# Block-decay attention ahead of two dense stages: the x products grouped by matmul shape, x in two PSUM banks

## The chip, the cores and the metric

The kernel runs on one core of a Trainium2 chip. Its engines work side by side: TensorE (PE, with its weight loads as PEld), VectorE (DVE), ScalarE (ACT), GpSimd (POOL), and SyncE (SP), which issues the DMAs. The metric is device time in microseconds of a whole execution; less is better.

## The reference

Attention with a decaying state over blocks, then two dense stages on its result:

```python
# q, k, v: [2, 8, 768, 64] float32; lam: [8], one decay per head
intra = einsum('bhic,bhjc->bhij', qb, kb) * Dmask        # Dmask = lam^(i-j) for j <= i, else 0
intra = einsum('bhij,bhjd->bhid', intra, vb)
inter = einsum('bhid,bhde->bhie', qb * lam_pow, kv_state)
out   = intra + inter
kv_state = lam_block * kv_state + einsum('bhsd,bhse->bhde', kb * rev_pow, vb)
...
x = attention as [1536 tokens, 512]
h = x @ w_in;  g = max(0.01 h, h);  y = g @ w_out         # w_in 512x2048, w_out 2048x512
a = y @ w1;  b = y @ w2;  out = (a * b) @ w3 @ w_out2      # 512x1024 twice, 1024x1024, 1024x512
```

The dense weights come as float64.

## The kernel before, in words

Tokens come in chunks of 128, twelve in all: chunks 0 to 5 are the first batch row, 6 to 11 the second. Chunks 0 and 6 start with an empty state (no state product), 5 and 11 hand none on (no outer product). Four chunks make a group of 512 tokens; three groups go through the dense stages. The eight heads lie as four pairs p with two heads j each; a pair fills 128 rows of 64 channels per head.

A chunk (`attention`, from line 345) has these steps. *Scores* (line 370): per pair and head a product with 64 contraction rows, the head's j going to PSUM buffer j. *Mask* (373, VectorE): scores times the decay table, for each j. *q decay* (382) and *k decay* (391, two instructions, one per j), on VectorE or GpSimd. *x products* (`outs`): per pair, line 408 multiplies the state (128x128, the two heads' 64x64 states on its diagonal, zeros elsewhere) with the decayed q, and line 411 adds v times the masked scores, one product per head, each to 64 of the 128 output rows. All of x of a chunk lies in one PSUM buffer. *x parts* (425 on ScalarE, 155 on VectorE): x is split into a rounded part and the rest, both kept for the dense stages. *Outer product* (436): per pair k x v as 128x128, of which the two diagonal 64x64 blocks are used. *Fade* (443, GpSimd): the old state, 128x512, times the decay. *Update* (453, or 455 for an empty state): two instructions, one per head of a pair, 64 rows each.

float32 products (attention) appear in the profile as two TensorE records each; the dense stages use rounded float32, one record each.

A step h(f) of the dense part is 12 products of 128x512 (line 467), y(f) as well (474); a group has 16 of each. Weights are loaded, converted from float64 words by ScalarE (227) and VectorE (231, 237, 251), split into rounded part and rest (151, 155), all beside the first group's products. The y step needs the activation of its h step: a scaled copy (502, ScalarE), a maximum (505, VectorE), a rounded part (482, ScalarE) and a rest (155, VectorE).

The order of all instructions is made ahead of time by `in_order`: each engine takes the first step in rank that is ready by the planner's own prices. Buffers come from rings handed out in turn. The ring `ps` has four PSUM buffers: scores take two, x products one, the outer product one, an h step one, held until the rest of its activation is made. `qd` and `kd` have one buffer each.

## Time and profile before

| what | value |
|---|---|
| median of three timed runs | 579.96 us (579.31 to 581.09) |
| span of the profiled execution, its own time as far as the profile gives it | 577.9 us |
| TensorE busy | 564.4 us, 98% |
| VectorE busy | 367.0 us, 64% |
| ScalarE busy | 316.5 us, 55% |
| GpSimd busy | 131.8 us, 23% |

Busy shares are means over stages with different limits. TensorE's matmuls are pipelined, so durations of single records overlap; the distance between the starts of one kind of block and the next tells what a block takes. An idle time is listed with what ended it.

### The profile page before, as it was taken

How to read it: one execution, taken by the hardware profiler on the slowest of the kernel's cores; microseconds unless marked ns; L12 is line 12 of the kernel's file. 1: busy time of each engine (PE TensorE's matmuls, PEld its weight loads, DVE VectorE, ACT ScalarE, POOL GpSimd, SP SyncE). 2: the span in 40 equal slices, each digit the busy share in tenths (PEclk: the TensorE clock that was granted, in tenths of full speed). 3: DMA queues.
4: the chain of work that ended last, by engine and by line, in shares of the span. 5: the costliest groups of instructions: out<-in, count | busy, mean ns of one | idle time of the engine just before them, and what ended most of it. 6: DMA issues, size and time to landing. Idle time of an engine off the chain costs nothing.

```text
span 577.9 us, 7411 instructions
## 1 busy us (share of the span) xinstructions
PE 564.4 (98%) x2752; PEld 458.3 (79%) x2752; DVE 367.0 (64%) x572; ACT 316.5 (55%) x531; POOL 131.8 (23%) x111
## 2 busy tenths in 40 slices
PE   5899999999999999999999999999999999999997
PEld 5668788787887878788888888888888888888885
DVE  7989899999544467553466999988435333333330
ACT  2366777677633346474466887887335333343332
POOL 2332202323223123112243241021002111111100
PEclk9999999999999999999999999999999999999999
DMA  8746745785210313110032444653001000020001
GB/s 301 278 151 218 254 148 186 245 283 200 75 70 19 109 56 110 47 63 0 1 113 69 146 146 152 212 182 111 0 1 67 7 0 1 0 74 0 1 1 73
DMA packets 19188, 60.25 MB, mean 104 GB/s; under 512 B 2256, under 2 KB 2256, under 8 KB 19152
## 3 DMA queue, kind: packets, MB, share of 16 engines
q1 hardware_dynamic: 19152, 59.78, 30.1%
q8 instruction: 21, 0.34, 0.2%
q14 instruction: 15, 0.12, 0.1%
HBM read 54.53 MB, written 5.24 MB: 103 GB/s over the span
## 4 chain that ended last, share of the span: by engine, by line
PE 88%; issue 4%; DVE 3%; DMA 2%; POOL 1%; SPq 0%; ACT 0%; DVEq 0%; POOLq 0%
PE ps L467 43%; PE acc L474 32%; PE ps L585 8%; PE ps L411 2%; PE ps L408 2%; PE ps L436 1%; DMA inp<-in_qkv_dram 1%; PE ps L370 1%; DMA yf<-in_qkv_dram 1%; POOL wp L155 1%; DVE kd L391 1%; DVE rp L231 0%; DVE u L237 0%; DVE state L453 0%; DVE xy L155 0%
## 5 line engine op out<-in xcount | busy, mean ns | idle before, releaser
L467 PE MATMUL ps<-xy,wp 128*128 128x512 f32 x1152 | 275.4, 390 | 0.9 <-DVE xy L155 0.9
L467 PEld LDWEIGHTS ps<-xy,wp 128*128 128x128 f32 x1152 | 215.5, 188 | 46.6 <-DVE xy L155 1.3
L474 PE MATMUL acc<-act,wp 128*128 128x512 f32 x576 | 140.6, 392 | 0.2 <-POOL wp L155 0.2
L474 PEld LDWEIGHTS acc<-act,wp 128*128 128x128 f32 x576 | 107.0, 188 | 24.6 <-issue 0.7
L155 DVE TENSOR_TENSOR act<-ps,act 128x512 fp32r<-128x512 f32 x72 | 49.6, 690 | 37.2 <-ACT act L482 37.1
L474 PE MATMUL acc<-wp,act 128*128 128x512 f32 x288 | 69.0, 389 | 0.0
L227 ACT ACTIVATE rp<-raw,bp 128x512 f32<-128x512 uint16 x72 | 55.0, 764 | 22.9 <-DVE f L251 11.1
L474 PEld LDWEIGHTS acc<-wp,act 128*128 128x128 f32 x288 | 54.1, 188 | 11.2
L227 ACT ACTIVATE rn<-raw,bn 128x512 f32<-128x512 uint16 x72 | 54.8, 763 | 14.6 <-DVE rp L231 10.4
L151 ACT CAST wp<-f_w 128x512 fp32r<-128x512 f32 x48 | 29.5, 621 | 55.4 <-PE ps L467 46.3
L482 ACT CAST act<-ps 128x512 fp32r<-128x512 f32 x72 | 42.1, 585 | 25.8 <-DVE ps L505 18.8
L151 ACT CAST wp<-f_in 128x512 fp32r<-128x512 f32 x48 | 29.8, 620 | 44.7 <-PE ps L467 42.1
L231 DVE SCALAR_TENSOR_TENSOR rp<-rp,rn 128x512 uint32<-128x512 f32 x72 | 51.3, 713 | 0.8 <-ACT rp L227 0.7
L155 POOL TENSOR_TENSOR wp<-f_w,wp 128x512 fp32r<-128x512 f32 x18 | 23.3, 1296 | 117.2 <-ACT wp L151 89.6
L155 DVE TENSOR_TENSOR wp<-f_in,wp 128x512 fp32r<-128x512 f32 x29 | 22.9, 790 | 42.6 <-ACT wp L151 42.5
L155 DVE TENSOR_TENSOR wp<-f_w,wp 128x512 fp32r<-128x512 f32 x30 | 23.0, 772 | 35.1 <-ACT wp L151 35.1
L237 DVE TENSOR_SCALAR u<-raw 128x512 uint32<-128x512 uint32 x72 | 43.2, 600 | 0.2
L155 POOL TENSOR_TENSOR wp<-f,wp 128x512 fp32r<-128x512 f32 x16 | 22.5, 1408 | 69.2 <-ACT wp L151 68.1
L155 POOL TENSOR_TENSOR wp<-f_in,wp 128x512 fp32r<-128x512 f32 x19 | 25.1, 1321 | 54.8 <-ACT wp L151 54.8
L505 DVE TENSOR_TENSOR ps<-ps,ta 128x512 f32<-128x512 f32 x48 | 33.3, 693 | 4.0 <-ACT ta L502 3.8
L151 ACT CAST wp<-f 128x512 fp32r<-128x512 f32 x40 | 24.9, 621 | 18.9 <-PE acc L474 5.6
L619 DVE TENSOR_TENSOR ps<-ps,ta 128x512 f32<-128x512 f32 x24 | 16.8, 698 | 28.9 <-PE ps L467 28.9
(71 smaller groups left out, 518.1 us busy)
## 6 DMA issues: line engine op xcount, KB each, us to landing
inp<-in_qkv_dram SPq DMA_DIRECT2D x20, 512.0 KB, 5.4
raw<-in_w_in_dram SPq DMA_DIRECT2D x16, 512.0 KB, 4.4
raw<-in_w_out_dram SPq DMA_DIRECT2D x16, 512.0 KB, 4.4
raw<-in_w3t_dram SPq DMA_DIRECT2D x16, 512.0 KB, 3.7
raw<-in_w_dram SPq DMA_DIRECT2D x16, 512.0 KB, 3.3
raw<-in_wo_dram SPq DMA_DIRECT2D x8, 512.0 KB, 3.7
f<-out SPq DMA_DIRECT2D x16, 256.0 KB, 2.6
out_dram<-f SPq DMA_DIRECT2D x12, 256.0 KB, 2.1
```

The costliest lines, as they stand in the source:

```text
L151: return lambda e: nc.scalar.copy(dst(), src())
L155: engines[e].tensor_tensor(out=dst(), in0=src(), in1=hi_().bitcast(F32), op=ALU.subtract)
L227: nc.scalar.activation(out=new(buf, [P, 512]), in_=top, func=AF.Relu, scale=8.0, bias=T_[bias])
L231: nc.vector.scalar_tensor_tensor(out=rp.tile.bitcast(U32), in0=rp.tile, scalar=32768.0, in1=rn.tile, op0=ALU.min, op1=ALU.add)
L237: nc.vector.tensor_scalar(out=new(u, [P, 512], U32), in0=mid, scalar1=2.0**-13, scalar2=2.0**19 - 1, op0=ALU.mult, op1=ALU.min)
L408: nc.tensor.matmul(ps[:, p, :], T_["state", n % 2][:, p, :], qd.tile[:, p, :], start=True, stop=False)
L467: nc.tensor.matmul(o, w(a)[:, cc * P : (cc + 1) * P], x(b, cc), start=k == 0, stop=k == 3 * NCC - 1)
L474: nc.tensor.matmul(o, st(a), mv(b), start=first and k == 0, stop=last and k == 2)
L482: nc.scalar.copy(buf.tile[:, 0, :], ps.tile)
L505: nc.vector.tensor_tensor(out=ps.tile, in0=ps.tile, in1=ta.tile, op=ALU.max)
L585: nc.tensor.matmul(ps.tile, w(a)[:, k * P : (k + 1) * P], wos[j // 2][:, 2 * (j % 2) + b, :], start=j == 0 and n == 0, stop=j == NF2 - 1 a ...
L619: lambda e: nc.vector.tensor_tensor(out=pb.tile, in0=pb.tile, in1=ta.tile, op=ALU.mult),
```

## The change

The x products come in two blocks: first all products with the state, as 64x64 pieces of the array (64 rows by the head j, 64 columns by the half t of the output), in an order in which four neighbours lie in four different pieces; then all products with v, whose neighbours alternate between the output halves. x lies in two PSUM buffers by the head's parity j, each 128x256; its parts are made by two instructions each on ScalarE and VectorE. The state holds the 64x64 blocks alone (128 rows by 4 x 64 columns), so the zeroed squares go, fade handles 256 columns instead of 512, and the update is one instruction of 128x256. The outer product is eight products of 64x64 instead of four of 128x128. The k decay is one instruction over all heads, from a small table (`last`) that two small copies on VectorE fill. The rows of w_in are permuted on the host to fit the new channel order of x. The planner's prices for these steps change, and with them the order.

```diff
@@ pool_consts, mask_table
-            T_["state", j] = const.tile([P, NPAIR, P], F32, tag="w34_7" if j else "state0", name=f"state{j}")
-            nc.gpsimd.memset(T_["state", j], 0.0)
-        T_["faded"] = const.tile([P, NPAIR, P], F32, name="faded")
+            T_["state", j] = const.tile([P, NPAIR, D], F32, name=f"state{j}")
+        T_["faded"] = const.tile([P, NPAIR, D], F32, name="faded")
...
+            if j == 0:
+                T_["last"] = const.tile([P, NPAIR, 2], F32, name="last")
+            nc.vector.tensor_copy(T_["last"][:, :, j : j + 1], T_["dm", j][:, :, CH - 1 : CH])
@@ attention
-        s = op({"pe": 1750}, scores, rank, [ld[0]], [*pss, *a], [inp])
+        s = op({"pe": 1000}, scores, rank, [ld[0]], [*pss, *a], [inp])
...
-                new(kd, [P, NPAIR, 2, D])
-                for j in range(2):
-                    engines[e].tensor_tensor(
-                        out=kd.tile[:, :, j, :],
...
-                        in1=T_["dm", j][:, :, CH - 1 : CH].to_broadcast([P, NPAIR, D]), op=ALU.mult,
+                engines[e].tensor_tensor(
+                    out=new(kd, [P, H, D]), in0=inp.tile[:, 2, :].rearrange("q (h d) -> q h d", d=D),
+                    in1=T_["last"].rearrange("q p j -> q (p j)").unsqueeze(2).to_broadcast([P, H, D]), op=ALU.mult,
+                )
...
-        px = Buf("ps")
+        px = [Buf("ps"), Buf("ps")]
+        heads = [(s, t, j) for s in range(2) for j in range(2) for t in range(2)]
...
-            for p in range(NPAIR):
-                if inter:
-                    nc.tensor.matmul(ps[:, p, :], T_["state", n % 2][:, p, :], qd.tile[:, p, :], start=True, stop=False)
-                for j in range(2):
-                    h = 2 * p + j
+            if inter:
+                for s, t, j in heads:
+                    p = 2 * s + t
                     nc.tensor.matmul(
-                        ps[j * D : (j + 1) * D, p, :], inp.tile[:, 3, h * D : (h + 1) * D], a[j].tile[:, p, :],
-                        start=not inter, stop=True,
+                        px[j].tile[half[t], s, :], T_["state", n % 2][half[j], p, :], qd.tile[half[j], p, :],
+                        start=s == 0, stop=False, skip_group_check=True,
                     )
+            for s, t, j in heads:
+                p = 2 * s + t
+                h = 2 * p + j
+                nc.tensor.matmul(
+                    px[j].tile[half[t], s, :], inp.tile[:, 3, h * D : (h + 1) * D], a[j].tile[:, p, :],
+                    start=not inter and s == 0, stop=True, skip_group_check=True,
+                )
...
-            {"pe": 2170 if inter else 1300}, outs, rank + 2, [*masked, ld[1], *need], [px, xs[g]] if c == 0 else [px],
+            {"pe": 1700 if inter else 1100}, outs, rank + 2, [*masked, ld[1], *need],
+            [*px, xs[g]] if c == 0 else px, [inp, *a, *([qd] if inter else [])],
...
-        o1 = op({"act": 520}, x_hi, rank + 2, [xo], [], [px, xs[g]])
+        for j in range(2):
+            part = lambda v, j=j: xs[g].tile[:, v, j::2, sl]
...
+            o1 = op({"act": 390}, x_hi, rank + 2, [xo], [], [px[j], xs[g]])
...
-                    nc.tensor.matmul(
-                        ps[:, p, :], kd.tile[:, p, :, :].rearrange("q h d -> q (h d)"),
-                        inp.tile[:, 3, p * P : (p + 1) * P], start=True, stop=True,
-                    )
+                    for j in range(2):
+                        h = 2 * p + j
+                        nc.tensor.matmul(
+                            ps[j * D : (j + 1) * D, p, :], kd.tile[:, h, :], inp.tile[:, 3, h * D : (h + 1) * D],
+                            start=True, stop=True,
+                        )
...
-                for j in range(2):
-                    r = slice(j * D, (j + 1) * D)
-                    st, ps = T_["state", (n + 1) % 2][r, :, r], pst.tile[r, :, r]
...
-                        nc.vector.tensor_tensor(out=st, in0=ps, in1=T_["faded"][r, :, r], op=ALU.add)
+                st = T_["state", (n + 1) % 2]
...
+                    nc.vector.tensor_tensor(out=st, in0=pst.tile, in1=T_["faded"], op=ALU.add)
```

How instructions move, at three places. The first is TensorE at chunk 9, from its scores on; before:

```order
L370 MATMUL ps<-inp 128x128 x8
L436 MATMUL ps<-inp,kd 128x128 x4
L467 MATMUL ps<-xy,wp 128x512 x12
L408 MATMUL ps<-qd,state_112 128x128
L411 MATMUL ps<-a_1789,inp 64x128
L411 MATMUL ps<-a_1790,inp 64x128
...
L474 MATMUL acc<-act,wp 128x512 x12
```

The same place with the change:

```order
L372 MATMUL ps<-inp 128x128 x8
L451 MATMUL ps<-inp,kd 64x64 x8
L480 MATMUL ps<-xy,wp 128x512 x12
L413 MATMUL ps<-qd,state_111 64x128 x8
L420 MATMUL ps<-a_1860,inp 64x128 x2
L420 MATMUL ps<-a_1861,inp 64x128 x2
...
L487 MATMUL acc<-act,wp 128x512 x12
```

The four turns of one state product and two v products have become a block of eight state products and a block of eight v products; the steps around them keep their places.

The second is TensorE from the v products of chunk 6 to the scores of chunk 7; before:

```order
L411 MATMUL ps<-a_822,inp 64x128
L411 MATMUL ps<-a_823,inp 64x128
L474 MATMUL acc<-act,wp 128x512 x12
L370 MATMUL ps<-inp 128x128 x8
L467 MATMUL ps<-xy,wp 128x512 x12
```

The same place with the change:

```order
L420 MATMUL ps<-a_835,inp 64x128 x2
L420 MATMUL ps<-a_836,inp 64x128 x2
L487 MATMUL acc<-act,wp 128x512 x24
L480 MATMUL ps<-xy,wp 128x512 x36
L487 MATMUL acc<-act,wp 128x512 x12
L480 MATMUL ps<-xy,wp 128x512 x12
...
L372 MATMUL ps<-inp 128x128 x8
```

Chunk 7's scores stand twelve h and y steps later behind chunk 6's x products than before, where one y step stood between.

The third is VectorE at the start, behind the decay tables (`yf` holds the inputs of chunks 0 and 1, `inp` those of later ones); before:

```order
L391 TENSOR_TENSOR kd<-yf_115,dm_118 128x4x64
L391 TENSOR_TENSOR kd<-yf_115,dm_123 128x4x64
L373 TENSOR_TENSOR a_132<-ps,dm_118 128x512
L373 TENSOR_TENSOR a_133<-ps,dm_123 128x512
L455 COPY state_112<-ps 64x4x64 x2
L391 TENSOR_TENSOR kd<-yf_128,dm_118 128x4x64
L391 TENSOR_TENSOR kd<-yf_128,dm_123 128x4x64
L155 TENSOR_TENSOR xy<-ps,xy 128x4x128
L373 TENSOR_TENSOR a_179<-ps,dm_118 128x512
L373 TENSOR_TENSOR a_180<-ps,dm_123 128x512
L453 TENSOR_TENSOR state_110<-ps,faded 64x4x64 x2
```

The same place with the change:

```order
L375 TENSOR_TENSOR a_133<-ps,dm_116 128x512
L375 TENSOR_TENSOR a_134<-ps,dm_123 128x512
L384 TENSOR_TENSOR qd<-yf_129,lpow 128x512
L155 TENSOR_TENSOR xy<-ps,xy 128x2x128 x2
L468 COPY state_111<-ps 128x256
L375 TENSOR_TENSOR a_185<-ps,dm_116 128x512
L375 TENSOR_TENSOR a_186<-ps,dm_123 128x512
L466 TENSOR_TENSOR state_110<-ps,faded 128x256
```

The k decays are gone from VectorE here; with the change GpSimd does them for every chunk, those of chunks 0 and 1 as its first work behind the constants, and the q decay of chunk 1 has come to VectorE.

## Rows read from the trace of the kernel before

**Rows 1.** The page's first part: busy time, share and count by engine.
```profile
PE 564.4 (98%) x2752; PEld 458.3 (79%) x2752; DVE 367.0 (64%) x572; ACT 316.5 (55%) x531; POOL 131.8 (23%) x111
```

**Rows 2.** By stage: us, PE, PEld, DVE, ACT, POOL, clock, DMA, GB/s.
```profile
5.69:33.33 27.64, 24.25 (x203) 18.26 (x203) 25.77 (x44) 10.82 (x17) 10.07 (x8) 1.00 0.78 295
33.33:140.00 106.67, 106.49 (x568) 84.05 (x570) 97.50 (x160) 77.96 (x129) 28.64 (x26) 1.00 0.65 221
140.00:242.00 102.00, 102.00 (x525) 82.22 (x524) 58.09 (x89) 49.69 (x87) 24.53 (x20) 1.00 0.20 68
300.00:577.90 277.90, 273.64 (x1205) 225.73 (x1203) 152.87 (x230) 146.09 (x247) 51.29 (x38) 1.00 0.19 67
```

**Rows 3.** What TensorE waited for: us in total, times, longest.
```profile
PE ps L467 <- DVE xy L155: 0.9, 1, 0.9
PE acc L474 <- POOL wp L155: 0.2, 1, 0.2
```

**Rows 4.** TensorE's timeline, 47 to 64 us: start, duration, operation, idle before it.
```profile
47.09 1.06 PE L436 MATMUL ps<-inp,kd 128*128 128x128 f32 x8
47.90 3.01 PE L474 MATMUL acc<-act,wp 128*128 128x512 f32 x12
50.75 2.88 PE L467 MATMUL ps<-xy,wp 128*128 128x512 f32 x12
53.56 1.16 PE L370 MATMUL ps<-inp 64*128 64x128 f32 x16
54.65 3.02 PE L474 MATMUL acc<-act,wp 128*128 128x512 f32 x12
57.51 2.89 PE L467 MATMUL ps<-xy,wp 128*128 128x512 f32 x12
60.23 0.39 PE L408 MATMUL ps<-qd,state 128*128 128x128 f32 x2
60.55 0.44 PE L411 MATMUL ps<-a,inp 128*64 128x128 f32 x4
60.92 0.49 PE L408 MATMUL ps<-qd,state 128*128 128x128 f32 x2
...
63.28 3.02 PE L474 MATMUL acc<-act,wp 128*128 128x512 f32 x12
```

**Rows 5.** TensorE's timeline around chunk 6, which has no state product.
```profile
99.39 1.09 PE L411 MATMUL ps<-a,inp 128*64 128x128 f32 x16
100.42 3.01 PE L474 MATMUL acc<-act,wp 128*128 128x512 f32 x12
```

**Rows 6.** Line 411: duration ns min/median/max, first and last start.
```profile
L411 PE MATMUL ps<-a,inp x160: 272/273/323, 19.7 to 240.6; 128*64 128x128 f32 x160
```

**Rows 7.** Groups of VectorE, 5.69 to 33.33 us: busy us, mean ns, idle before.
```profile
L155 DVE TENSOR_TENSOR xy<-ps,xy 128x512 fp32r<-128x512 f32 x4 | 2.8, 693 | 0.1
L453 DVE TENSOR_TENSOR state<-ps,faded 64x256 f32<-64x256 f32 x6 | 2.5, 417 | 0.0
L391 DVE TENSOR_TENSOR kd<-yf,dm 128x256 f32<-128x256 f32 x4 | 2.4, 636 | 0.6 <-DMA yf<-in_qkv_dram 0.6
L391 DVE TENSOR_TENSOR kd<-inp,dm 128x256 f32<-128x256 f32 x4 | 1.5, 412 | 0.0
L455 DVE COPY state<-ps 64x256 f32<-64x256 f32 x2 | 0.8, 422 | 0.9 <-PE ps L436 0.9
```

**Rows 8.** Groups of ScalarE and GpSimd, whole execution.
```profile
L425 ACT CAST xy<-ps 128x512 fp32r<-128x512 f32 x12 | 7.0, 586 | 16.9 <-PE ps L411 16.7
L443 POOL TENSOR_TENSOR faded<-state,lpow 128x512 f32<-128x512 f32 x8 | 10.1, 1259 | 8.4 <-DVE state L453 7.5 <-DVE state L455 0.9
L382 POOL TENSOR_TENSOR qd<-inp,lpow 128x512 f32<-128x512 f32 x5 | 7.0, 1390 | 18.9 <-PE ps L408 12.8 <-DMA inp<-in_qkv_dram 5.2 <-issue 1.0
```

**Rows 9.** Timeline, all engines: end of an h step, last reader of its buffer.
```profile
107.31 3.22 PE L474 MATMUL acc<-act,wp 128*128 128x512 f32 x12
...
111.37 0.69 DVE L155 TENSOR_TENSOR act<-ps,act 128x512 fp32r<-128x512 f32 x1 [1.22 <-ACT act L482]
```

More of the change, by code (lines that the diff above doesn't have):

```diff
@@ L375, in mask @@
             )
-        s = op({"pe": 1750}, scores, rank, [ld[0]], [*pss, *a], [inp])
-        masked = [op({"dve": 602}, mask(j), rank + j, [s, tables[j]], [], [pss[j], a[j]]) for j in range(2)]
+        s = op({"pe": 1000}, scores, rank, [ld[0]], [*pss, *a], [inp])
+        masked = [op({"dve": 640}, mask(j), rank + j, [s, tables[j]], [], [pss[j], a[j]]) for j in range(2)]
         q_op = k_op = None
@@ L399, in attention @@
             x_ops[g] = []
-        px = Buf("ps")
+        px = [Buf("ps"), Buf("ps")]
+        heads = [(s, t, j) for s in range(2) for j in range(2) for t in range(2)]
         def outs(e):
-            ps = new(px, [P, NPAIR, CH])
+            for b in px:
+                new(b, [P, 2, CH])
             if c == 0:
                 new(xs[g], [P, 2, NCC, T], F32R)
-            for p in range(NPAIR):
-                if inter:
-                    nc.tensor.matmul(ps[:, p, :], T_["state", n % 2][:, p, :], qd.tile[:, p, :], start=True, stop=False)
-                for j in range(2):
-                    h = 2 * p + j
+            half = [slice(0, D), slice(D, P)]
+            if inter:
+                for s, t, j in heads:
+                    p = 2 * s + t
@@ L444, in fade @@
                     out=T_["faded"], in0=T_["state", n % 2],
[L445 removed]
+                    in1=T_["lpow"][:, :, CH - 1 : CH].to_broadcast([P, NPAIR, D]), op=ALU.mult,
                 )
             def update(e):
[L449 to L459 removed]
+                st = T_["state", (n + 1) % 2]
+                if inter:
+                    nc.vector.tensor_tensor(out=st, in0=pst.tile, in1=T_["faded"], op=ALU.add)
+                else:
+                    nc.vector.tensor_copy(st, pst.tile)
+            so = op({"pe": 800}, outer, rank + 2, [k_op, ld[1]], [pst], [inp, kd])
+            fo = op({"pool": 700}, fade, rank + 2, [last_st[n - 1]]) if inter else None
+            last_st[n] = op({"dve": 420}, update, rank + 2, [so, fo, x_done.get(n - 1), tables[2]], [], [pst])
         x_done[n] = xo
```

31 lines of the change are left out of this document (12 added, 19 removed).

## Prediction

> **What bounds the kernel now.** I read the page's busy shares first, then the busy time by stage, then what TensorE waited for, then its timeline around single chunks, last the groups of VectorE in the first stage. TensorE is busy 98% of the span [rows 1]. By stage [rows 2], from 33.33 us on it is busy with hardly a break: 106.49 of 106.67 us, 102.00 of 102.00, and 273.64 of the last 277.90. Its waits for other engines in the whole execution are short [rows 3]: 0.9 us for the last part of x and 0.2 us for a weight. So after 33.33 us each microsecond of TensorE work removed is a microsecond of time, as long as nothing else turns late.
>
> The stage ahead of it, 5.69 to 33.33 us, holds chunks 0 to 3 and the first weights. TensorE is busy 24.25 of its 27.64 us, but VectorE 25.77 [rows 2]: VectorE sets the pace there. The candidate for being late next is VectorE again from 33.33 to 140 us, where weights are converted beside the first group's products: 97.50 of 106.67 us, 91%. From 140 to 242 us it has only 58.09 of 102, so there TensorE's gains are safe.
>
> **Products of x, the main term.** In the timeline [rows 4] chunk 5's x products run from 60.23 to 63.28 us: 3.05 us, as four turns of one 128x128 state product (2 records, 0.32 us to the next start in the first turn) and two products with v (4 records, 0.37 us). Afterwards there are two blocks. The block with v is the one that chunk 6, which has no state product, shows already: 16 records from 99.39 to 100.42, 1.03 us [rows 5]. The block with the state is 16 records on 64x64 pieces, which no row shows. The row of chunk 6 has 16 records on two pieces of the array, 1.09 us from the first start to the last end; take off the median of one record, 0.27 [rows 6], and the starts span 0.82 us, which is 7 steps of two records at 0.11 to 0.12. Until the next kind starts, 1.03 - 8 x 0.11 = 0.15 us more goes by. Bounds for the state block:
> - four pieces at once: 4 steps of 0.11 and the 0.15, so 0.60 us;
> - only two at once, as in chunk 6: 1.03 us;
> - none at once: 16 steps of 0.11 and the 0.15, 1.9 us.
>
> I take 0.60. The nearest rows are the scores, which pair two row pieces (16 records in 1.09 us, 53.56 to 54.65 [rows 4]), and chunk 6, which pairs two column pieces; the new block has both splits, and its neighbours in the order lie in four different pieces.
>
> A rule speaks against it. The Trainium skill (TensorE: Matmul & The Clock Gate, section "Wait — 56ns, not 53.3ns?") gives a floor of some 25 ns between matmul starts, and 62 ns per matmul where the sequencer decodes them in software. By the second the block would take 16 x 62 ns and 0.15, 1.14 us, about the two-at-once case. The 16 starts in 0.82 us of chunk 6 are 51 ns apart, under 62, so this trace disagrees with the second floor; whether 27 ns is reached no row here shows.
>
> Entering a tiled block costs something that the mixed order did not pay: a 12-matmul step takes 2.72 us ahead of the old x products (57.51 to 60.23) and 2.81 ahead of the scores (50.75 to 53.56). I charge 0.09. The exit (2.86 against 2.72) is paid before and after alike. So a chunk with a state saves 3.05 - 0.09 - 0.60 - 1.03 = 1.33 us (0.90 at two at once, 0.03 at none). Chunks 4, 5, 7, 8, 9, 10 and 11 do so behind 33.33 us: 7 x 1.33 = 9.3 us, bounds 0.2 and 9.3. Chunk 6 saves nothing here.
>
> **The outer product (k v).** Now 4 products of 128 columns, 8 records, 0.81 us (47.09 to 47.90 [rows 4]); then 8 products of 64 columns, 16 records, two pieces. Below: half of chunk 6's step per pair, 8 x 0.055 and 0.15, 0.60 us; above: chunk 6's 1.03. With 0.09 of entry the change is -0.12 to +0.31 us; I take +0.1. Six of them lie behind 33.33 us (chunks 4, 6, 7, 8, 9, 10): +0.6 us, bounds -0.7 and +1.9.
>
> **The first stage.** VectorE's list up to the last rest of x of chunk 3 changes so, from the groups of that stage [rows 7]: the eight halves of k decay go to GpSimd (2.4 and 1.5 us); the four state updates of two halves each (2.5 and 0.8 us) become three single ones ahead of that point, as wide per partition as one half, 0.42 each, so 3.3 - 1.3 = 2.0 saved; the four rests of x (2.8 us, 0.69 each) become eight of half the width. Such a half costs between 0.35 (half of 0.69) and the 0.42 of an update, which also reads PSUM; at 0.41 that is +0.5. Two copies of 4 columns for the table have no row like them; I count 0.1 for both, between 0 and an update's 0.42 each. Net 3.9 + 2.0 - 0.5 - 0.1 = 5.3 us off 25.77. That is the upper bound of what this stage gives. The lower is near 0, since three new links appear: k decay runs on GpSimd at the price of a q decay there, 1.39 us [rows 8], against 0.8 for a pair on VectorE, and it has one buffer, so chunk 1's waits for chunk 0's outer product; x takes two of the four PSUM buffers, so that the next scores' second bank waits until x has been read out; GpSimd and VectorE stretch each other (k decay on VectorE has a mean of 0.64 in one group and 0.41 in the other). Cover for these: TensorE's own work in this stage shrinks by three x blocks. I take 4.0.
>
> **What the stage from 33.33 to 140 us gives back.** TensorE's work shrinks by 4 x 1.33 = 5.3 us there (chunks 4, 5, 7, 8). VectorE's hardly does: three updates at 0.42 less, chunk 3's update more, five rests of x at +0.12: about -0.3. Then 97.2 us of VectorE stand against 101.4 of TensorE, 96%. The order shows also that chunk 7 is placed later, behind a stretch of h and y steps without attention, where conversion asks most of VectorE. Working for it: fade handles half the columns (1.26 us on GpSimd now [rows 8]), and the k decay is one instruction. I charge 2.0 us of new TensorE waits, between 0 and 5. ScalarE's half more (x as two copies; one of 128x512 is 0.59 [rows 8]; two halves cost 0 to 0.3 more) lies beside TensorE's steps and costs nothing while ScalarE has 77.96 of 106.67 us [rows 2].
>
> **Sum against the profiled execution.** 577.9 - 4.0 - 9.3 + 0.6 + 2.0 = 567.2 us of span. The median of the timed runs, 579.96, lies 2.06 above the span; so 569.3, forecast 569.
>
> **Rivals.**
> - *Two pieces at once only.* The state block takes 1.03: 7 x 0.43 = 3.0 us less gain, 572.3. For it: only pairs are seen in any row. Against: row splits and column splits pair each by themselves.
> - *VectorE takes the gain.* The conversion stage gives back all that TensorE saves in it, 5.3 instead of 2.0, and the first stage brings only 2.5: 569.3 + 3.3 + 1.5 = 574.1. For it: 91% busy already. Against: in 106.67 us TensorE waited 0.2. The Trainium skill (TensorEngine Tiling (Array Packing), section "PSUM Bottleneck") has this rule: tiling speeds up the products, not the readout of PSUM, which may become the bottleneck; the trace agrees so far as VectorE is the nearest to full.
> - *Slower, by the ring of four PSUM buffers.* A chunk takes five instead of four. The extra one can put x's second bank behind an h step that has just ended. An h step's buffer comes free late: its matmuls end at 107.3 and its last reader at 111.37 + 0.69 = 112.06, 4.75 us [rows 9], of which a y step between covers 2.7. So up to 2 us a time. At one such wait per chunk behind 33.33 us (8), of 2 us each, in place of the 2.0 charged: 569.3 + 16 - 2 = 583. It decides from 1.6 us per chunk (12.6 / 8). Against: the mask, which TensorE awaits anyway, frees the same buffers in most turns of the order.
> - *Better still.* No waits, the first stage at 5.3, outer products at their lower bound: 569.3 - 2.0 - 1.3 - 1.3 = 564.7.
>
> **How the numbers follow.** Chances: forecast 0.58 (566.5 to 571.5), two at once 0.15, VectorE 0.15, slower 0.06, better 0.06. A range of 565 to 576 leaves out the slow case and edges, about 0.15 to 0.2. The likeliest case's own range is 566.5 to 571.5. About 0.3% (1.7 us) can be told from no change here: faster 0.91; slower 0.05, most of the ring's case; same 0.04, the rest of it and VectorE's case together with two at once.
>
> **What would show it.** In the profile afterwards: the state block as 16 records within 0.6 us (or 1.03), x products of a chunk 1.6 to 1.7 us instead of 3.05; the outer product 0.6 to 1.0; the first h step near 29 us, where it is 33.33 now; TensorE's waits for VectorE or GpSimd between there and 136 us summing to some 2 us; from then on the same steps, shifted. Wrong would be: 16 records with starts 0.05 us apart; a first h step at 32 us or later; TensorE waits of over 5 us before 136 us; waits that end in the readout of x.

## The result, and the profile after

The kernel with the change takes 575.13 us (median of 4 runs, 573.35 to 575.3) against 580.08 (4 runs) in the same rounds: ratio 0.9905, interval 0.989 to 0.992. The gain is 5.0 us where 11 were forecast. The profiled execution after has a span of 573.6 us and was one of 575.3.

The page's busy line, then the stages (the columns of [rows 2]); the lines answer to [rows 1] and [rows 2]:

```profile
PE 553.4 (96%) x2912; PEld 452.4 (79%) x2912; DVE 358.9 (63%) x570; ACT 316.6 (55%) x543; POOL 129.7 (23%) x105
```

```profile
5.69:33.33 27.64, 22.75 (x254) 19.34 (x255) 23.92 (x39) 11.18 (x22) 12.95 (x11) 0.88 0.77 293
33.33:140.00 106.67, 100.77 (x592) 80.04 (x591) 96.76 (x166) 78.75 (x134) 22.62 (x18) 0.97 0.65 218
140.00:242.00 102.00, 102.00 (x627) 82.43 (x627) 56.30 (x89) 50.12 (x90) 26.48 (x21) 1.00 0.21 72
```

From 33.33 to 140 us TensorE has lost its unbroken row, 100.77 of 106.67 us where it was 106.49, and in this stage and the one ahead of it the granted clock is below 1. What it waited for, in place of [rows 3] (us in total, times, longest):

```profile
PE ps L480 <- DVE xy L155: 5.1, 1, 5.1
PE ps L413 <- DVE xy L155: 2.8, 1, 2.8
PE ps L451 <- POOL kd L391: 1.2, 1, 1.2
```

The blocks themselves, TensorE's timeline (start, duration, operation) in the place of [rows 4]:

```profile
43.32 0.67 PE L413 MATMUL ps<-qd,state 64*64 64x128 f32 x16
43.91 1.09 PE L420 MATMUL ps<-a,inp 128*64 128x128 f32 x16
44.94 3.02 PE L487 MATMUL acc<-act,wp 128*128 128x512 f32 x12
47.88 0.69 PE L451 MATMUL ps<-inp,kd 128*64 128x64 f32 x16
48.50 3.02 PE L480 MATMUL ps<-xy,wp 128*128 128x512 f32 x12
```

The state block takes 0.59 us (43.32 to 43.91), the whole of x 1.62 where it was 3.05, the outer product 0.62 where it was 0.81. So the x blocks went as forecast, and the outer product better than that. Where the time is can be read at the scores of chunks 9 and 10, ahead of which both kernels have done the same work on TensorE. Before, then after:

```profile
179.48 1.16 PE L370 MATMUL ps<-inp 64*128 64x128 f32 x16
...
206.64 1.16 PE L370 MATMUL ps<-inp 64*128 64x128 f32 x16
```

```profile
180.22 1.16 PE L372 MATMUL ps<-inp 64*128 64x128 f32 x16
...
205.78 1.16 PE L372 MATMUL ps<-inp 64*128 64x128 f32 x16
```

From one to the other it was 27.16 us and is 25.56: each chunk gives 1.60. But chunk 9's scores themselves start 0.74 us *later*. Four chunks with a state (4, 5, 7 and 8) lie between 33 us and there, and all of their gain and the first stage's is gone; only chunks 9, 10 and 11 gained. From chunk 9's scores to the end of the span it is 393.4 us in this kernel and, within 0.1, in all its variants below that keep the two x buffers. So the start of chunk 9's scores ("S9" below) measures the disputed part by itself.

It went at two places. The first is the first stage. Before, from chunk 4's scores to its x products:

```profile
30.62 1.16 PE L370 MATMUL ps<-inp 64*128 64x128 f32 x16
31.71 0.73 PE L467 MATMUL ps<-xy,wp 128*128 128x512 f32 x2
33.33 5.29 PE L467 MATMUL ps<-xy,wp 128*128 128x512 f32 x22 [0.88 <-DVE xy L155]
38.45 0.39 PE L408 MATMUL ps<-qd,state 128*128 128x128 f32 x2
```

After, from chunk 3's x products to chunk 4's scores:

```profile
24.97 1.36 PE L413 MATMUL ps<-qd,state 64*64 64x128 f32 x16 [2.76 <-DVE xy L155]
26.26 1.97 PE L420 MATMUL ps<-a,inp 128*64 128x128 f32 x16
28.02 1.07 PE L451 MATMUL ps<-inp,kd 128*64 128x64 f32 x16
29.02 6.83 PE L480 MATMUL ps<-xy,wp 128*128 128x512 f32 x24
35.78 1.16 PE L372 MATMUL ps<-inp 64*128 64x128 f32 x16
```

Chunk 3's x products wait 2.76 us until chunk 2's rests free two of the four PSUM buffers, and then the blocks take nearly twice their time: 1.29, 1.76 and 1.00 us from start to start, where 0.59, 1.03 and 0.62 stood above. The second place is behind chunk 6's x products:

```profile
78.56 1.09 PE L420 MATMUL ps<-a,inp 128*64 128x128 f32 x16
79.59 6.13 PE L487 MATMUL acc<-act,wp 128*128 128x512 f32 x24
85.56 2.88 PE L480 MATMUL ps<-xy,wp 128*128 128x512 f32 x12
93.55 8.58 PE L480 MATMUL ps<-xy,wp 128*128 128x512 f32 x24 [5.11 <-DVE xy L155]
101.96 2.88 PE L487 MATMUL acc<-act,wp 128*128 128x512 f32 x12
```

Two h steps wait 5.11 us for chunk 6's rests on VectorE, and their 24 matmuls then take 8.41 us, against 5.44 for two steps at 2.72. Stretches of the same trace show the clock behind both waits (columns as in the stages; the clock is the last but two):

```profile
24.90:29.00 4.10, 4.03 (x48) 3.63 (x48) 4.10 (x9) 1.09 (x3) 0.00 (x0) 0.50 0.55 211
```

```profile
93.55:97.00 3.45, 3.45 (x8) 2.77 (x9) 3.45 (x6) 1.68 (x3) 2.31 (x2) 0.50 0.63 212
97.00:99.00 2.00, 2.00 (x6) 1.52 (x6) 2.00 (x5) 1.90 (x4) 0.00 (x0) 0.50 0.75 241
99.00:101.96 2.96, 2.96 (x13) 2.37 (x12) 2.93 (x6) 2.96 (x6) 0.16 (x1) 0.88 0.80 275
```

0.50 is 1.2 of 2.4 GHz. The second wait costs 5.11 and then 2.97 us more. Behind the first wait the clock doesn't fall in every execution: raw6, a run below with the same instruction lists, waits 2.75 us there and keeps the full clock:

```profile
24.90:29.00 4.10, 3.42 (x51) 2.48 (x52) 4.10 (x9) 1.91 (x5) 0.67 (x1) 1.00 1.01 404
```

Why chunk 6's rests come at 92.99, while ScalarE had made its copies by 82.1, three views show: SyncE's queue, one row of ScalarE, three of VectorE:

```profile
77.79 0.33 SPq L224 DMA_DIRECT2D raw<-in_w_in_dram  x1
79.74 0.33 SPq L356 DMA_DIRECT2D inp<-in_qkv_dram  x1
80.54 0.33 SPq L224 DMA_DIRECT2D raw<-in_w_out_dram  x1
```

```profile
86.76 0.75 ACT L229 ACTIVATE rn<-raw,bn 128x512 f32<-128x512 uint16 x1 [2.80 <-DMA raw<-in_w_out_dram]
```

```profile
88.70 0.69 DVE L155 TENSOR_TENSOR wp<-f_in,wp 128x512 fp32r<-128x512 f32 x1 [2.06 <-ACT wp L151]
...
92.99 0.74 DVE L155 TENSOR_TENSOR xy<-ps,xy 128x256 fp32r<-128x256 f32 x2
93.66 0.41 DVE L468 COPY state<-ps 128x256 f32<-128x256 f32 x1
```

A weight's load leaves at 80.54, behind a load of chunk 8 that had waited 1.6 us for chunk 6's x products. What the weight's load itself waited for last is its raw buffer, which VectorE read until about 80.5. ScalarE waits for the load until 86.76, some 6.2 us from its issue, with two loads of chunk 8 (79.74 and 80.92) on their way beside it. VectorE waits until 88.70, and from there VectorE's list has eight conversion steps to go through (88.70 to 92.39) ahead of the rests. Which link of this counts is what the experiments ask.

### The profile page after: what moved, and what is told of

Read it like the earlier page. It is cut to its first block, busy times and chain, and to the rows that moved or that the text cites. A ratio compares the mean times of both kernels' runs of the same rounds, so it can differ in the third digit from the quotient of the medians.

```text
span 573.6 us, 7733 instructions
## 1 busy us (share of the span) xinstructions
PE 553.4 (96%) x2912; PEld 452.4 (79%) x2912; DVE 358.9 (63%) x570; ACT 316.6 (55%) x543; POOL 129.7 (23%) x105
## 4 chain that ended last, share of the span: by engine, by line
PE 87%; DVE 7%; DMA 3%; ACT 2%; issue 1%; SPq 0%; ACTq 0%; DVEq 0%
PE ps L480 43%; PE acc L487 32%; PE ps L598 8%; PE ps L372 2%; PE ps L420 2%; DVE rp L233 1%; DVE u L239 1%; DMA raw<-in_w_out_dram 1%; DMA raw<-in_w_in_dram 1%; DVE f_in L253 1%; DVE wp L155 1%; DVE a L375 1%; PE ps L451 1%; DMA yf<-in_qkv_dram 1%; PE ps L413 1%
## 5 line engine op out<-in xcount | busy, mean ns | idle before, releaser
L480 PE MATMUL ps<-xy,wp 128*128 128x512 f32 x1152 | 279.2, 394 | 5.8 <-DVE xy L155 5.1
L480 PEld LDWEIGHTS ps<-xy,wp 128*128 128x128 f32 x1152 | 218.3, 190 | 52.9 <-ACT rn L229 5.5
L229 ACT ACTIVATE rn<-raw,bn 128x512 f32<-128x512 uint16 x72 | 54.9, 764 | 15.2 <-DVE rp L233 10.5
L155 DVE TENSOR_TENSOR wp<-f_in,wp 128x512 fp32r<-128x512 f32 x36 | 26.2, 731 | 45.9 <-ACT wp L151 45.7
L155 POOL TENSOR_TENSOR wp<-f,wp 128x512 fp32r<-128x512 f32 x17 | 23.8, 1402 | 79.3 <-ACT wp L151 72.6
L515 ACT ACTIVATE ta<-ps 128x512 f32<-128x512 f32 x48 | 28.6, 596 | 8.0 <-PE ps L480 7.9
```

The lines of the kernel that those rows point to most:

```text
L155: engines[e].tensor_tensor(out=dst(), in0=src(), in1=hi_().bitcast(F32), op=ALU.subtract)
L229: nc.scalar.activation(out=new(buf, [P, 512]), in_=top, func=AF.Relu, scale=8.0, bias=T_[bias])
L480: nc.tensor.matmul(o, w(a)[:, cc * P : (cc + 1) * P], x(b, cc), start=k == 0, stop=k == 3 * NCC - 1)
L515: nc.scalar.activation(out=new(ta, [P, T]), in_=ps.tile, func=AF.Copy, scale=0.01)
```

## The experiments

Each was timed beside the kernel before in the same rounds; the ratio is to that. "Interval" is from the start of chunk 6's x products to the h steps behind its rests; TensorE has 9.9 us of other work in it (78.56 to 88.44 above), the rest is wait; "moved" says that the wait is at another place. S9, interval and wait are of one profiled execution, the time is a median of 4 or 5 runs (10 for the fourth row). The fourth row is b_raw6 in the text.

| run | time, us (range) | ratio [95%] | S9 | interval, wait |
|---|---|---|---|---|
| before | 580.08 (579.31–581.09) | 1 | 179.48 | |
| after | 575.13 (573.35–575.3) | 0.9905 [0.989, 0.992] | 180.22 | 14.99, 5.11 |
| grouped | 576.45 (575.74–578.78) | 0.9936 [0.991, 0.996] | 179.29 | |
| before, six raw | 579.86 (579.18–581.85) | 0.9993 [0.998, 1.001] | 181.34 | |
| same_piece | 574.25 (572.65–574.54) | 0.9881 [0.986, 0.990] | 177.51 | 14.30, 4.42 |
| no_max | 575.0 (574.09–575.7) | 0.9899 [0.988, 0.992] | 179.01 | 15.30, 5.42 |
| rest6 | 575.7 (574.41–576.14) | 0.9908 [0.989, 0.993] | 179.36 | moved |
| raw6 | 573.6 (572.11–576.48) | 0.9889 [0.986, 0.992] | 177.02 | 13.91, 4.04 |
| raw6_no_max | 574.93 (571.76–576.35) | 0.9903 [0.987, 0.994] | 181.16 | 14.08, 4.19 |
| raw6_rest6 | 571.85 (570.38–572.43) | 0.9848 [0.983, 0.987] | 176.64 | moved |
| rest6_h8 | 573.59 (572.18–574.38) | 0.9881 [0.986, 0.990] | 178.81 | moved |
| raw6_rest6_h8 | 571.06 (570.9–571.61) | 0.9846 [0.983, 0.986] | 175.88 | moved |
| rest2 | 573.34 (572.06–573.37) | 0.9878 [0.986, 0.989] | 177.00 | 14.14, 4.26 |
| raw6_late | 572.94 (572.6–575.74) | 0.9869 [0.984, 0.990] | 180.64 | 12.85, 2.95 |
| light | 570.11 (568.16–571.47) | 0.9805 [0.978, 0.984] | 175.14 | 14.83, 5.16 |
| raw6_late8 | 571.2 (571.15–572.72) | 0.9839 [0.982, 0.986] | 176.06 | 12.85, 2.97 |
| raw6_late8_light | 567.33 (566.11–568.01) | 0.9759 [0.974, 0.978] | 172.91 | 11.75, 2.09 |
| best3 | 573.94 (572.92–575.41) | 0.9877 [0.986, 0.990] | 178.49 | moved |
| best2 | 573.83 (573.35–574.01) | 0.9872 [0.986, 0.989] | 178.64 | moved |
| best4 | 570.59 (569.74–571.42) | 0.9822 [0.980, 0.984] | 175.58 | moved |

Executions of one kernel differ with the mean clock that they were granted: raw6 took 572.11 us at 0.997 (the profiled one), 573.68 at 0.991 and 576.48 at 0.988, the kernel after 573.35 at 0.991 and 575.3 at 0.988 (the profiled one). same_piece differs from the kernel after in the order of eight products alone and has 574.25 us, S9 177.51, interval 14.30; rest2, with the same lists around chunk 6, has 14.14. So a difference of 1 us in time or interval, or of 3 us in S9, decides nothing by itself; executions of like clock are compared where it matters.

**Does the order of the state block matter?** same_piece puts each two neighbouring products in the same 64x64 piece:

```diff
-                for s, t, j in heads:
+                for s, t, j in sorted(heads, key=lambda x: (x[2], x[1], x[0])):
```

> The changed kernel with the eight state products of a chunk issued so that neighbours lie in the same 64x64 piece of the array; the same products otherwise. Theory A (four neighbours in four pieces run at once): the state block takes 1.0 to 1.9 us instead of 0.59, and seven to nine chunks cost 3 to 9 us more: 578 to 584 (575.1 with the order of the change). Theory B (the order within the block does not matter, records of 64 columns are short anyway): 0.6 us, 575.

The block takes 0.62 us (42.51 to 43.13) against 0.59, as theory B had it: the order is no part of it.

```profile
42.51 0.69 PE L413 MATMUL ps<-qd,state 64*64 64x128 f32 x16
43.13 1.09 PE L420 MATMUL ps<-a,inp 128*64 128x128 f32 x16
```

**What does grouping alone give?** grouped is the kernel before with its four state products of 128x128 ahead of the eight with v, in one x buffer and in before's order:

```diff
             for p in range(NPAIR):
-                if inter:
-                    nc.tensor.matmul(ps[:, p, :], T_["state", n % 2][:, p, :], qd.tile[:, p, :], start=True, stop=False)
...
+            if inter:
+                for p in range(NPAIR):
+                    nc.tensor.matmul(
+                        ps[:, p, :], T_["state", n % 2][:, p, :], qd.tile[:, p, :], start=p == 0, stop=False,
+                        skip_group_check=True,
+                    )
```

> The kernel before with one part of the change: the four 128x128 products with the state come first, then the eight with v; x stays in one PSUM buffer, all else and the planner's order stay. Theory A (the block order is what saves, the lost part is the second PSUM buffer): a chunk's x products take 0.9 to 1.1 us for the state block and 1.03 for the v block, 2.0 to 2.1 instead of 3.05; seven chunks behind 33 us save 6.7 to 7.4 us, no new wait of TensorE over 1 us: 572 to 573.5 (580.1 before). Theory B (VectorE is full from 33 to 140 us): the three chunks behind 140 us save 3 us, the four ahead of it nothing: 576.5 to 577.5.

From chunk 9's scores (179.29) to chunk 10's (205.41) it takes 26.12 us: grouping gives 1.04 of the 1.60 us per chunk. And here too nothing is left by chunk 9's scores, 179.29 against 179.48, with before's order and one x buffer per chunk. So the second x buffer isn't needed for the gain ahead of chunk 9 to vanish, and the time is theory B's, 576.45. But it goes at other places than in the kernel after: chunk 5's scores stand 1.36 us later than before (54.92 against 53.56), behind a wait of 2.65 us for the rests of x at 35.73, and from there to chunk 9's scores it gains 1.55 us of the 3.1 that its three chunks with a state save, while y steps wait 1.4 us for weights. That VectorE's full list takes the gain, theory B's reason, is not shown by this.

**Is it the ring of PSUM buffers?** rest6 takes the planner's list and moves chunk 6's two rests and its state update forward on VectorE, to where their inputs are ready by the planner:

```diff
+        for n, moved in early.items():
+            if n == 6:
+                for m in moved:
...
+                    seq.insert(k, seq.pop(i))
```

> The changed kernel with three instructions of VectorE moved: the two rests of x of chunk 6 and its state update stand where their inputs are ready by the planner's clock, ahead of the weight conversions behind which the planner put them. Theory A (PSUM ring): the 5.1 us that TensorE waits ahead of the second of three h steps, at 88.4 us, is the wait for PSUM buffers that chunk 6 still holds; with the move it falls to under 1.5 us (what is left is that step's weight), the two h steps behind it take 5.6 us instead of 8.4 because TensorE's clock does not fall, and the time is 567.5 to 570 (575.1 before the move). Theory B (VectorE is full): the same work in another order; the wait turns up at the weights of the next steps, the waits of TensorE between 33 and 140 us still sum to some 5 us, and the time is 573.5 to 575.5.

The wait goes, and another comes behind the three h steps:

```profile
85.98 8.62 PE L482 MATMUL ps<-xy,wp 128*128 128x512 f32 x36
98.53 5.44 PE L489 MATMUL acc<-act,wp 128*128 128x512 f32 x12 [3.93 <-ACT act L497]
```

Freeing the ring alone brings nothing (575.7, 0.2 above theory B's range): the next thing that TensorE needs is late as well.

**Is it VectorE's capacity?** no_max leaves out the maximum of the leaky rectifier.

```diff
-            nc.vector.tensor_tensor(out=ps.tile, in0=ps.tile, in1=ta.tile, op=ALU.max)
+            pass
```

> The changed kernel without the maximum of the leaky step (48 instructions of VectorE at 0.69 us, 16 of them in the first group's stage, 11 us of 97 there); the scaled copy on ScalarE stays, and the order of everything else. It leaves out the leaky rectifier. Theory B (VectorE is full): TensorE's waits between 33 and 140 us vanish, the clock stays up, 566 to 568. Theory A (PSUM ring): only the two or three maxima that stand between chunk 6's x products and its rests on VectorE shorten the wait of 5.1 us, by 1.4 to 2.1; 3.0 to 3.7 of it stay, the clock falls as before, and the time is 571 to 573.5.

The stage 33.33 to 140 us of no_max, columns as before:

```profile
33.33:140.00 106.67, 99.79 (x592) 79.27 (x591) 87.07 (x151) 78.06 (x134) 19.97 (x17) 0.97 0.69 225
```

VectorE falls to 82%, and the wait stays at 5.42. Both theories missed: one wanted the waits gone, the other this one shorter by 1.4 us or more. A busy share of the stage doesn't decide; a list that waits in one place does (VectorE waits 2.36 us for a weight at 88.30 here).

**Are the loads late?** raw6 gives the raw weights six buffers for four, lists unchanged; b_raw6 does that to the kernel before; raw6_rest6 joins raw6 and rest6.

```diff
-        r: ctx.enter_context(tc.tile_pool(name=r, bufs=n, **({"space": PS} if r in ("ps", "acc") else {})))
+        r: ctx.enter_context(tc.tile_pool(name=r, bufs=n + 2 * (r == "raw"), **({"space": PS} if r in ("ps", "acc") else {})))
```

> The kernel after, with six buffers for the raw weights where there were four, and every engine's list of instructions unchanged. Theory C (between 33 and 110 us the loads of the weights set the pace: a load is issued only when VectorE has let go of the raw buffer four slices back, and it lands 3 to 6 us later): the 5.11 us wait ahead of the three h steps near 93.55 falls under 1 us, their 24 matmuls take 5.6 us again instead of 8.41, and the time is 567 to 569. Theory D (ScalarE's and VectorE's own work, in the order in which it is listed, sets the pace; the loads only follow it): the wait stays within 1 us of 5.1 and the time at 574 to 575.5.

> The kernel before, with six raw buffers instead of four and its lists unchanged. Both theories: TensorE already ran without a break from 33.33 us on, so nothing is to be had there; 579 to 580.5. Under theory C up to 1 us may come off the first stage, where loads also wait for the ring.

> The same six raw buffers, and also chunk 6's two rests of x and its state update moved forward on VectorE as in the earlier run with that edit (575.7). Theory C together with the ring of PSUM buffers: loads were why the wait only moved to the y step at 98.5, so now both waits are gone, and the time is 566 to 569. Theory D: 574.5 to 576, with the 3.9 us wait at 98.5 still there.

The wait falls only to 4.04, where kernels with four buffers and the same lists around chunk 6 have 4.26 to 5.11, and at like clock the time is that of the kernel after (573.68 against 573.35 at 0.991). Theory C missed, and theory D is nearer. SyncE's queue in raw6 shows why six buffers help so little:

```profile
70.84 0.33 SPq L224 DMA_DIRECT2D raw<-in_w_in_dram  x1
78.89 0.33 SPq L356 DMA_DIRECT2D inp<-in_qkv_dram  x1
79.33 0.37 SPq L224 DMA_DIRECT2D raw<-in_w_out_dram  x1
```

It stands still for 8 us: chunk 8's load waits for the buffer that chunk 6 holds until its x products are done (77.72 to 78.75), and the weights' loads stand behind it. The weight of 79.33 landed at 84.82, and ScalarE waited 1.69 us for it. raw6_rest6 takes 1.75 us less than raw6 (at a clock of 0.997, 570.38 against 572.11), where rest6 on four buffers gained nothing; that fits late loads and the ring covering for each other. Its 571.85 lies between the two theories' ranges, and a wait of 2.40 us for the ninth h tile is left. The kernel before is the same with six buffers.

**Order, or amount of conversion work?** rest6_h8 and raw6_rest6_h8 also move the next late thing, the four steps that make the ninth h tile ready, ahead of some ten conversion steps, and its h step ahead of a y step (numbers are places in the planner's list: step, and the step behind which it goes). raw6_no_max joins raw6 and no_max (without the maximum).

```diff
+        for i, k in [(336, 332), (345, 319), (350, 324), (354, 327), (359, 337)]:
+            seq.remove(planned[i])
+            seq.insert(seq.index(planned[k]) + 1, planned[i])
```

> The kernel after with chunk 6's rests and state update moved forward on VectorE as in the earlier run (575.7), and now also the four steps that make the ninth h tile ready for its y step moved forward past some ten conversion steps on ScalarE and VectorE; four raw buffers. Theory E (the lists of ScalarE and VectorE are written in an order in which conversions of later weights stand ahead of the two things TensorE needs next, and with loads late they run some 7 us behind): the 3.9 us wait at 98.5 goes, some of it comes back at the next weight because loads wait for the raw buffers; 571 to 573.5. Theory F (the amount of conversion work up to there, in whatever order, sets the pace): 575 to 576.5, the wait moves once more.

> The same lists with six raw buffers, so that loads are early. Theory E: neither wait is left, the clock stays up between 80 and 105 us, and 571.85 falls by the 2.4 us wait and the 1.9 us that its y step lost to the clock: 567 to 568.5. Theory F: 571 to 572.5, with a new wait of 2 us or more for a weight before 110 us.

> The kernel after with six raw buffers and without the maximum of the leaky rectifier on VectorE (that part of the computation is left out): loads and VectorE's load are both relieved, while each alone left the wait (4.04 us with six buffers, 5.42 without the maximum). Theory E and theory F alike: chunk 6's rests come some 3 to 4 us sooner, since VectorE runs without a break ahead of them once loads are early, so the wait ahead of the three h steps falls under 1 us and the time to 567 to 569.5. If ScalarE or anything else bounds the chain, the wait stays over 2.5 us and the time over 571.5.

On four buffers the move gives 2.1 us (573.59, 0.1 above theory E's range); on six only 0.8, which is within the scatter, and theory F's time. There the long waits are gone, but each h step now starts with one matmul and a short wait for its weight, and steps come 6.67 us apart (97.41 to 104.08) where two at 2.72 make 5.44:

```profile
97.41 0.49 PE L482 MATMUL ps<-xy,wp 128*128 128x512 f32 x1
98.19 2.79 PE L482 MATMUL ps<-xy,wp 128*128 128x512 f32 x11 [0.28 <-DVE wp L155]
100.85 3.01 PE L489 MATMUL acc<-act,wp 128*128 128x512 f32 x12
104.08 0.50 PE L482 MATMUL ps<-xy,wp 128*128 128x512 f32 x1 [0.22 <-ACT wp L151]
```

TensorE waits for the conversions of weights there, a little at each step. raw6_no_max missed what theories E and F had in common, a wait under 1 us: it was 4.19, and what came true is the branch "ScalarE or anything else". VectorE wasn't late by its own load there; it waited in turn for the weight held up behind chunk 8's load (ScalarE waited 1.85 us for it at 88.08).

**The first stage.** rest2 moves one ScalarE and two VectorE conversion steps behind chunk 2's copies and rests:

```diff
+        for i, k in [(59, 63), (60, 69), (64, 60)]:
```

> The kernel after, where in the first stage chunk 2's two copies of x on ScalarE go ahead of one conversion step, and its two rests of x on VectorE ahead of two. Theory of the PSUM ring (chunk 3's x products wait 2.76 us for chunk 2's rests to free two of four buffers, and the clock falls behind that wait): the wait falls under 1 us, the first h step starts near 26.5 instead of 29.0 and its 24 matmuls take 5.6 to 6.2 us instead of 6.8. If the 33 to 110 us stretch is paced by the conversions, as the earlier runs say, the whole time nevertheless falls by less than 1.5 us: 573.5 to 575.5; if it is paced by TensorE, 571 to 572.5.

The wait of 2.76 us became one of 0.54, with one of 1.65 for the mask behind it; the clock in 5.69 to 33.33 us is 1.00, and chunk 4's scores start at 33.83 instead of 35.78. Most of that is the clock: from chunk 3's scores to chunk 4's it takes 12.50 us, 13.03 in raw6, whose clock there is 1.00 as well with chunk 2's steps where they were, and 14.73 in the kernel after. So the move itself gives 0.5 us. The time, 573.34, is 1.8 us below that of the kernel after and 0.9 below same_piece, between the two ranges; whether the conversions take back what the first stage gains it doesn't decide.

**The queue, and the conversions' own work.** raw6_late moves the loads of chunks 6, 7 and 8 back in SyncE's list; light leaves out the second ScalarE step on a weight's top bits and the VectorE step that joins them; best3 is raw6_late with rest6 and rest2, best2 that with the h8 moves.

```diff
+        for i, k in [(158, 201), (180, 158), (214, 250), (238, 214), (237, 263), (281, 394), (296, 281)]:
```

```diff
+                if bias == "bp":
+                    nc.scalar.activation(
+                        out=new(buf, [P, 512]).bitcast(U32), in_=top, func=AF.Relu, scale=8.0, bias=T_[bias]
+                    )
...
-            nc.vector.scalar_tensor_tensor(
-                out=rp.tile.bitcast(U32), in0=rp.tile, scalar=32768.0, in1=rn.tile, op0=ALU.min, op1=ALU.add
-            )
+            pass
```

> The kernel after with six raw buffers, and with the loads of chunks 6, 7 and 8 moved back in SyncE's list behind weights' loads that they held up (and one q decay of chunk 7 moved back on GpSimd behind chunk 6's products); all else as in the run with six raw buffers (573.6). Theory G (weights' loads stand in SyncE's queue behind a chunk's load that waits for its buffer, so the conversions lack data in 33 to 90 us): ScalarE no longer waits for raw data before 95 us, the wait ahead of the three h steps falls from 4.0 to under 1.5 us, 569 to 571.5. Theory F (the amount of conversion work): wait within 1 us of 4.0, 573 to 574.5.

> The kernel after with less work per converted weight slice: without the second of the two ScalarE steps on the top bits and without the VectorE step that joins them (the sign of a weight is left out); per slice 0.67 us less on ScalarE and 0.60 less on VectorE, some 20 slices before 93 us. Lists, rings and loads as they are. Theory F (the work of the conversions sets the pace): the wait ahead of the three h steps goes, and the time falls to 566 to 569.5. Theory G (the loads set the pace): raw buffers come free no sooner relative to the queue that is blocked by chunk loads, a wait of 2.5 us or more stays and the time is 571.5 to 574.

> Six raw buffers, late chunk loads, chunk 6's rests forward and chunk 2's rests forward. Theory G: the single gains add up (rests of chunk 2: 1.8; rests of chunk 6 with six buffers: 1.8 more than six buffers alone; late loads 2 to 3): 566.5 to 569. Theory F: the conversions take back what the first stage gains: 570 to 572.

> As the one with late loads and both pairs of rests forward, and also the ninth h tile's steps forward on ScalarE and VectorE with its h step ahead of the y step before it. Theory G: within 1 us of the kernel without that, 566 to 569. Theory F: 570 to 572.

raw6_late shortens the interval to 12.85 and the wait to 2.95, between the two theories. But moving chunk 6's load too made a new wait of 1.81 us, at 65.02, for a weight that GpSimd finishes: ahead of that, GpSimd waits 7.85 us for chunk 6's load to make a k decay. So best3 and best2, which carry it, fell short (573.94 and 573.83, above both ranges). light splits the two: chunk 4's scores start at 30.91, so the first stage hangs on the conversions (3.2 us sooner than in raw6 at the same clock, 4.9 sooner than in the kernel after), but the interval is 14.83, with four VectorE steps, some 2.4 us, gone from the list in it. ScalarE waits for the load instead:

```profile
83.09 0.75 ACT L230 ACTIVATE rp<-raw,bp 128x512 uint32<-128x512 uint16 x1 [4.00 <-DMA raw<-in_w_out_dram]
```

The interval isn't set by the conversions' work while a load is late in it; the time, 570.11, lies between the two ranges, as the first stage gained all the same.

raw6_late8 moves chunk 8's loads alone, raw6_late8_light has the lighter conversions as well, best4 is raw6_late8 with rest6 and rest2:

```diff
+        for i, k in [(281, 394), (296, 281)]:
```

> The kernel after with six raw buffers and with only chunk 8's two loads moved back in SyncE's list, behind seven weights' loads. In the run with six buffers chunk 8's load stood until chunk 6's x products were done (78.9 us), the weight's load behind it landed at 84.8, and ScalarE waited 1.69 us for it. Theory H (two limits close together: that load, and right behind it VectorE's list): ScalarE's wait there goes, VectorE works without a break from the masks to the rests, the interval from the start of chunk 6's x products to the h steps falls from 13.9 to about 12.8 us, the wait from 4.0 to about 3; 572 to 573.5. Theory G (the loads alone): the wait falls under 1 us, 568 to 570.

> The same, and with the lighter conversions (one ScalarE step and one VectorE step less per weight slice, the sign of a weight left out), which alone took 570.1 with a wait of 5.16 us left. Theory H: both limits are moved, the interval falls under 10.5 us, the wait under 1 us, and its h steps run at full clock: 563 to 566. If something else holds the interval, the wait stays over 2.5 us: 567.5 to 570.

> Six raw buffers, chunk 8's loads late, chunk 6's rests and chunk 2's rests forward; no part left out. Theory H: under the 571.85 of six buffers with chunk 6's rests forward by the 1.8 us that chunk 2's rests gained and by up to 1 us for the load, 569 to 571. If the conversions' pace takes it all back: 571.5 to 573.

The h steps behind chunk 6's rests, raw6_late8, then raw6_late8_light:

```profile
90.64 7.33 PE L480 MATMUL ps<-xy,wp 128*128 128x512 f32 x24 [2.97 <-DVE xy L155]
```

```profile
87.51 7.31 PE L481 MATMUL ps<-xy,wp 128*128 128x512 f32 x24 [2.09 <-DVE xy L155]
```

With chunk 8's load out of the way the interval is 12.85, as theory H had it (12.8), and the time 0.8 us below its range; VectorE shows no idle between 72 and 94 us, so its list is the second limit. The edit takes chunk 8's loads away twice, from ahead of the weight's load in the queue and from beside it on the way; which of the two counts it doesn't tell, and on four buffers it wasn't tried. With both limits moved the interval falls to 11.75 and the time to 567.33. That is the right direction and less than expected (under 10.5; 563 to 566): in the shorter list VectorE waits 0.15 to 0.35 us at a time for ScalarE. best4 takes 570.59 us, ratio 0.9822 [0.980, 0.984], in theory H's range: the lowest median of the kernels that leave nothing out, with raw6_rest6_h8 and raw6_late8 within 0.6 us of it. Its h steps run without a break at full clock, and one longer wait is left there, for the ninth h tile:

```profile
86.17 8.33 PE L482 MATMUL ps<-xy,wp 128*128 128x512 f32 x36
96.42 3.06 PE L489 MATMUL acc<-act,wp 128*128 128x512 f32 x12 [1.91 <-ACT act L497]
```

## Why the prediction was right in part and wrong in sum

- *State block 0.60, v block 1.03, x 1.33 less per chunk*: right, 0.59 and 1.03. The prediction's reason for the state block, four neighbours in four pieces, isn't borne out: same_piece has 0.62. So the size came out right by luck, and whether pieces run at once stays open. The 16 records take 37 ns each. By the second floor that the Trainium skill gives (TensorE: Matmul & The Clock Gate, "Wait — 56ns, not 53.3ns?"), 62 ns for each, the block would have taken 1.14 us. Counted per record this trace disagrees with that floor; counted per product (eight, 74 ns each) it doesn't, and by the same count chunk 6's records, on which the prediction turned it down, don't either.
- *Outer product +0.1 each*: too high by some 0.4. It takes 0.62 for 0.81; a chunk gives 1.60 in all, so 0.27 beside the 1.33, and not 1.23.
- *First stage 4.0*: wrong, about 1.5. The mark chosen was bad: the 33.33 us read as the first h step is its third matmul, behind chunk 4's scores, which the change puts behind the h steps. So the first h step at 29.02, where "near 29" was forecast, is no success. At equal work (24 h matmuls and chunk 4's scores done) it is 38.45 before and 36.9 after. The 2.76 us wait for two of four PSUM buffers was named as a new link, priced low, and the half clock behind it wasn't priced: 0.70, 0.73 and 0.38 us on the three blocks, and 1.1 on the two h steps (6.76 for 2.86 and 2.81). In raw6, with the same wait at the full clock, the same mark stands at 35.2, a gain of 3.3: of the 2.9 us that the clock cost, other waits take back 1.2 there.
- *The stage from 33.33 to 140 us gives back 2.0, bounds 0 and 5*: the step that failed most. It gave back 5.8 us of waits, 5.11 of them at one place, and 3.0 of clock, a term that the sum didn't have. The bound took VectorE's share (96%) as the risk. The runs show a chain in its place: a weight's load that comes late, ScalarE's and VectorE's conversions behind it, chunk 6's rests behind those in VectorE's list, and h steps that need the PSUM buffers the rests free. From the start of chunk 6's x products it takes 14 to 15 us (raw6 to after), and TensorE has 9.9 us of work meanwhile. What makes the load late is shown with six raw buffers: chunk 8's load, which waits in SyncE's queue for chunk 6's x products; without it the interval is 12.85, and with lighter conversions too 11.75. With four, as in the kernel after, the load's last wait is for its raw buffer, and what it then spends 6.2 us on isn't shown. No run that left the rests where they were took away the last 2.09 us of the wait. The prediction had seen that the order puts chunk 7 behind a stretch of h and y steps, but not read SyncE's list against it. Its own signs of being wrong, waits of over 5 us before 136 us that end in the readout of x, are what the profile shows.
- *Sum*: 1.5 + 7 x 1.33 + 6 x 0.27 - 8.8 = 3.6 us of span, measured 577.9 - 573.6 = 4.3; 0.7 us stays unassigned, 0.5 of it behind chunk 9's scores, and the profiled execution was the slowest of its kernel's four.
- *Rival "VectorE takes the gain", 574.1*: nearest in time, but no_max shows that it isn't VectorE's load alone; the order of its list and what it waits for count. *Rival "ring of PSUM buffers"*: such waits were there, twice and not eight times, and longer than 2 us each; the rests forward at chunk 2 gain some 0.5 us at like clock, at chunk 6 nothing by themselves.

Left open: how much the kernel before would gain from lighter conversions wasn't tried, so the 567.33 isn't compared with a like kernel; and kernels with the same lists in the first stage take 13.03 us (raw6) to 14.73 (after) from chunk 3's scores to chunk 4's, with the clock at 1.00 or 0.50 behind the same wait; why it falls in one execution and not in another no run shows.

## What to carry to other kernels

When an engine that was never idle gets less work, look for what it kept waiting without harm: read the in-order queues of loads for entries that wait for that very engine, with other loads behind them. Mark progress at a place ahead of which both kernels have done the same work, not at the first row of a kind. Price a wait on TensorE with the clock behind it: here 5.1 us of wait cost 8.1. Before two variants are compared, look at the granted clock of their executions: here it moved one kernel's time by more than most edits did.

## What the runs showed of the hardware

- Behind a wait TensorE ran at a granted clock of 0.50 for some 5 us (after, 93.55 to 99). In every run with a wait of 2.1 to 5.4 us ahead of the two h steps their row is 7.29 to 8.58 us long, where such a row is 5.60 long at the full clock (after, at 558.79); the loss hardly follows the wait (7.31 behind 2.09 us, 7.34 behind 4.26). Behind 2.75 us in the first stage the clock stayed at 1.00 in raw6 and was 0.50 in the kernel after (24.90 to 29.00).
- Grouping matmuls by shape is worth 1.04 us per chunk without any smaller piece (grouped): seven changes between 128x128 and 128x64 within the block become one.
- A VectorE step of 0.68 us took 1.70 beside GpSimd steps (after, at 93.99, beside GpSimd's 1.29 from 93.85 and 1.07 from 95.10).
